# Attention with a gated bilinear branch: masked Q tiles copied out of one SBUF evacuation, and a third quad with four more VectorE tiles

**Chip and metric.** The kernel runs on one core of one Trainium2 chip. The metric is the device time of one execution in microseconds (us), as the median of several executions; a profile of one execution stands beside it. "Span" is the time from the first to the last instruction in a profile; the device time is 1.6 to 1.8 us longer in the profiled runs shown first.

## The reference, cut to what matters

```python
# x: [1, 2048, 512] bf16; 32 heads of 16; F = 1376
g = sigmoid((x * gate_w).sum(-1, keepdims=True))
q, k, v = split(x @ wqkv)                       # per head, Dh = 16
p = softmax(einsum("bhqd,bhkd->bhqk", q, k) * Dh ** -0.5)
a = einsum("bhqk,bhkd->bhqd", p, v) ... @ wo
b = ((x @ w_gate) * (x @ w_up)) @ w_down
return g * a + (1 - g) * b
```

There are 32 heads with 2048 x 2048 scores each. In tiles of 128 keys by 512 queries that makes 2048 tiles whose exponential is wanted. This is most of the work.

## The kernel before

The program is a list scheduler. While it is built, it plays the five engines forward with fixed durations (a "plan") and emits each instruction in the order in which the plan starts it. Each engine's program on the chip is its list in that order, with waits on semaphores in it. So any change of a duration, a buffer or a seed gives a new order of everything.

A "quad" is a group of query block and heads with 64 score tiles (32 quads). ScalarE takes 48 tiles of a quad, as true exps, two or three tiles wide ("pairs" and "triples"). VectorE takes 16: it makes a 16-bit integer approximation straight from PSUM, then VectorE or GpSimd add three constants to it ("shift copies"), and TensorE averages the four versions in the PV product. In the quads of HBQ, VectorE takes 20 and ScalarE 44. The PV product is that of the probabilities with the values. A "bank" is a piece of PSUM that matmuls write, "bank X" the one named psX; an "evacuation" reads a finished result out of it, and this program lets TensorE use it again only after that.

```python
    HBQ = [24, 30]                    # quads in which VectorE takes four more tiles
    NMAIN = 54                        # 128x512 cells for probabilities
...
    # query block: projected into a PSUM bank, evacuated twice, each time times a mask
    for p in range(2):
        ev_q[c, b, p] = add("dve", [last, o_mask] + q_last.get((c - 1, b), []),
            lambda v, p=p: v.tensor_scalar(QM[:, p, b, :], bk.ap, mask[:, p : p + 1], None, ALU.mult),
            0.66, prio=2, cb=lambda k: bk.readers.append(k))
...
    # in gen_step: shift copies of VectorE run when the plan has GpSimd free, and GpSimd waits for them
    if eng in ("dve", "pool") and (best is None or best.prio > CPR):
        if eng == "pool" or lock["pool"] <= t:
            c = try_copy(eng, t)
            if c is not None:
                if eng == "dve":
                    lock["op"] = c
                elif lock["op"] is not None:
                    c.deps.append(lock["op"])
...
    SEED = 3                          # shifts the planned positions of the projections and MLP ("fills")
```

Note what the ordering of shift copies does: GpSimd waits by a semaphore for VectorE's copies (in the profile before 112.4 us in 89 waits, its largest). VectorE does not wait for GpSimd; that side rests on the plan's times alone.

The softmax here doesn't subtract the row's maximum and nothing guards it: scores larger than these inputs give would overflow.

Of the kernel before, what the change touches and what calls it, by code (L numbers as in the profile page):

```python
# [6 lines left out]
BF16 = mybir.dt.bfloat16  # L7
# [189 lines left out]
def _build(nc, A_x, A_wqkv, A_wo, W_gate, W_up, W_down, gate_w, out):  # L197
# [10 lines left out]
    NB = 4  # L208
    FT = (F + 127) // 128
    FW = [min(128, F - 128 * f) for f in range(FT)]  # L210
    NMAIN = 54
    C_V = NMAIN
    C_H = C_V + 4
    C_D = C_H + FT
# [1 line left out]
    NM = NQ * NCH  # L216
    RA = 24
    VW = 18
    HBQ = [24, 30]
    HB = sorted({(m % NQ) // 2 for m in HBQ})  # L220
    XU = {1: 3, 4: 2, 7: 1, 10: 0}
    XI = {1: 0, 4: 1, 7: 2, 10: 3}
# [12 lines left out]
    with ExitStack() as stack:  # L235

        def sb(name, shape, dt):
            return stack.enter_context(nc.sbuf_tensor(name, shape, dt))
# [17 lines left out]
        OX = sb("OX", [128, 2, 512], BF16)  # L256
        hT = sb("hT", [128, FT, 512], BF16)
        usb = sb("usb", [128, 2, 512], BF16)
        ost = sb("ost", [128, 2, D], BF16)
        oraw = sb("oraw", [128, NO, 512], F32)  # L260
        rb = sb("rb", [128, NO, 512], F32)
# [15 lines left out]
        psO = stack.enter_context(nc.psum_tensor("psO", [128, 512], F32))  # L277

        P = _Plan()
        clock = {"pe": 0.9, "act": 0.9, "dve": 0.9, "pool": 0.9, "sp": 0.9}  # L280
        qs = {e: [] for e in clock}

# [28 lines left out]
        def now(eng, deps, fn, occ, **kw):  # L311
            k = _Task(eng, deps, fn, occ, **kw)
            r = ready(k)
            assert r is not None
            return run_task(k, max(clock[eng], r))
# [62 lines left out]
        )  # L378
        m0 = now("dve", [], lambda v: v.memset(mask[:], 0.0), 0.1)
        for j in range(4):  # L380
            m0 = now("dve", [m0], lambda v, j=j: v.memset(mask[32 * j : 32 * j + 16, 0:1], QS), 0.1)
        o_mask = now("dve", [m0], lambda v: v.tensor_scalar(mask[:, 1:2], mask[:, 0:1], -1.0, QS, ALU.mult, ALU.add), 0.1)
        o_one = now("pool", [], lambda g: g.memset(VS[:, :, :, Dh:VW], 1.0), 0.95)
        o_vone = o_one
        o_sel = now("pool", [], lambda g: g.memset(sel[:], 0.0), 0.3)
# [212 lines left out]
        def f_q(c, b, pos):  # L598
            packs = [
                (  # L600
                    lambda bk, kt=kt: col(
                        bk.ap, wq[:, kt, b * 128 : (b + 1) * 128], xT[:, kt, c * 512 : (c + 1) * 512], kt == 0, kt == KD - 1
                    ),
                    PACK,
                    "c",
                )
                for kt in range(KD)
            ]

            def evac(bk, last):  # L610
                bk.need += 2
                for p in range(2):
                    ev_q[c, b, p] = add(
                        "dve",
                        [last, o_mask] + q_last.get((c - 1, b), []),
                        lambda v, p=p: v.tensor_scalar(QM[:, p, b, :], bk.ap, mask[:, p : p + 1], None, ALU.mult),  # L616
                        0.66,
                        prio=2,
                        cb=lambda k: bk.readers.append(k),
                    )  # L620

            def deps():
                if c and not q_done.get((c - 1, b)):
                    return [None]
                return [d_wq[b]] + xdep(c)

            return Fill(f"q{c}{b}", packs, deps, evac, pos)
# [74 lines left out]
        def f_gate(pos):  # L702
            def mk(bk, kt):
                def fn(e, q):
                    return e.matmul(
                        bk.ap[32 * q : 32 * q + 1, :],
                        gw[:, kt : kt + 1],
                        xT[:, kt, q * 512 : (q + 1) * 512],
                        start=(kt == 0),
                        stop=(kt == KD - 1),  # L710
                        tile_position=(0, 32 * q),
                        skip_group_check=True,
                    )

                return pack4(fn)

            packs = [(lambda bk, kt=kt: mk(bk, kt), PACK, "c") for kt in range(KD)]
            grow = ost.rearrange("p a b -> p (a b)").bitcast(F32)

            def evac(bk, last):  # L720
                bk.need += 1
                e0 = None
                e0 = add("dve", [last], lambda v: v.tensor_copy(grow, bk.ap), 0.61, prio=3, cb=lambda k: bk.readers.append(k))
                e1 = add(
                    "sp",
                    [e0],
                    lambda e: e.dma_start(gscr, grow[0:128:32, :]),
                    0.1,
                    lat=3.0,
                    stream="dgl",  # L730
                    dma=True,
                )
                gsrc = bass.AP(gscr.tensor, gscr.offset, [[1, 128], [128, T]])
                e2 = add(
                    "sp",
                    [e1],
                    lambda e: e.dma_start(gex[:, :], gsrc, allow_slow_non_contiguous=True),
                    0.5,
                    lat=9.0,
                    stream="dgl2",  # L740
                    dma=True,
                )
                e3 = add("act", [e2], lambda a: a.activation(gval[:], gex[:], ACT.Exp, scale=-1.0), 0.1, lat=0.33)
                e4 = add("dve", [e3], lambda v: v.tensor_single_scalar(gden[:], gval[:], 1.0, ALU.add), 0.1)
                e5 = add("dve", [e4], lambda v: v.reciprocal(gval[:], gden[:]), 0.1)
                ogate["g"] = add("dve", [e5], lambda v: v.tensor_scalar(omg[:], gval[:], -1.0, 1.0, ALU.mult, ALU.add), 0.1)

            return Fill("gate", packs, lambda: [d_gw] + xt_all + d_x[1:], evac, pos)
# [3 lines left out]
        def f_u(c, f, pos):  # L752
            w = FW[f]
            packs = [
                (
                    lambda bk, kt=kt: col(
                        bk.ap, wu[:, kt, f * 128 : f * 128 + w], xT[:, kt, c * 512 : (c + 1) * 512], kt == 0, kt == KD - 1
                    ),
                    PACK,
                    "c",  # L760
                )
                for kt in range(KD)
            ]
            n = c * FT + f

            def evac(bk, last):
                bk.need += 1
                ocopy[n] = add(
                    "dve",
                    [last, omul.get(n - 2), o_xt[0]],  # L770
                    lambda v: v.tensor_copy(usb[0:w, n % 2, :], bk.ap[0:w, :]),
                    0.6,
                    prio=3,
                    cb=lambda k: bk.readers.append(k),
                )

            def deps():
                if n >= 2 and n - 2 not in omul:
                    return [None]
                return [d_wu] + xdep(c)  # L780

            return Fill(f"u{c}.{f}", packs, deps, evac, pos)

        def f_g(c, f, pos):
# [13 lines left out]
            def evac(bk, last):  # L798
                bk.need += 1
                omul[n] = ev_h[c, f] = add(  # L800
                    "dve",
                    [last, ocopy[n], oend.get((c - 1, 3)), o_xt[0]],
                    lambda v: v.tensor_tensor(hT[0:w, f, :], bk.ap[0:w, :], usb[0:w, n % 2, :], ALU.mult),  # L803
                    0.6,
                    prio=3,
                    cb=lambda k: bk.readers.append(k),
                )

# [12 lines left out]
        def f_d(c, tt, pos):  # L821
# [12 lines left out]
            def evac(bk, last):  # L834
                oend[c, tt] = last
                bk.need += 1
                ev_b[c, tt] = add(
                    "dve",
                    [last, ogate["g"], bfree.get(t - 4) if t < T - 4 else None],
                    lambda v: v.tensor_scalar(b_ap(t), bk.ap, omg[:, t : t + 1], None, ALU.mult),  # L840
                    0.66,
                    prio=3,
                    cb=lambda k: bk.readers.append(k),
                )

# [12 lines left out]
        def combine(t, bank_ap, last, cb=None):  # L858
# [4 lines left out]
                [last, ev_b[c, tt], ogate["g"]] + ([o_out.get(t - 2)] if t < T - 4 else []),  # L863
                lambda v: v.scalar_tensor_tensor(o_dst, bank_ap, gval[:, t : t + 1], b_ap(t), ALU.mult, ALU.add),
                0.66,
                prio=3,
                cb=cb,
            )
            bfree[t] = k
# [196 lines left out]
            return len(pr["p1"]) == len(pr["u"]) and (len(pr["u"]) == 2 or pr.get("last"))  # L1066

        def even(c):
            return len(c) < 3 or all(b - a == c[1] - c[0] for a, b in zip(c, c[1:]))

        def try_copy(eng, t):
            best = None
# [254 lines left out]
        for c in range(NCH - 1):  # L1327
            for b in range(NB):
                fills.append(f_q(c + 1, b, UA0[NQ * c + 2 * b + 2] + 30.0))
        SEED = 3  # L1330
        for i, f in enumerate(fills):
            if f.pos > 0:
                f.pos += ((SEED * 7919 + i * 104729 + SEED * i * 31) % 97) / 97.0 * 6.0 * (SEED > 0)
# [86 lines left out]
        FA1 = 99  # L1420
        LA0 = 0
        LA1 = 1
        XF = -99
        FB = 2
        AOH = 0.057
        M4 = 1
        _build.m4 = 0
# [46 lines left out]
        def pe_step():  # L1474
# [15 lines left out]
            if can and tE <= t:  # L1490
# [24 lines left out]
                        use3 = "d"  # L1515
                if use3 == "d":
                    db.append(s[2])
                if use3 != "f" and bank_free(so[2], t) and lag >= LA1 and not (st["mq"] and so[2] is DB) and st["slot"] == 0:
                    db.append(so[2])
                nmax = 3 if use3 == "a" else 2  # L1520
                djs, dus, dbs = [], [], []
# [67 lines left out]
        def filler(t, can=True):  # L1589
# [22 lines left out]
            if fin and pv is None and st["fill"] is None and wts and fready(wts[0], t):  # L1612
                for bk in tbs:
                    if bank_free(bk, t):
                        start_fill(wts[0], bk, wts)
                        break
            if pv is not None and (nfree < NF or st["fill"] is None or fin):
                do_pv(pv, t)
                return True
            if st["fill"] is not None:  # L1620
# [299 lines left out]
```

## Time and profile before

| | before |
|---|---|
| time, median of 3 | 716.47 us (716.22 to 717.03) |
| profiled execution | 714.12 us, span 712.5 us |
| ScalarE (ACT) busy | 700.3 us, 98% |
| TensorE (PE) busy | 683.8 us, 96% |
| VectorE (DVE) busy | 641.4 us, 90% |
| GpSimd (POOL) busy | 428.4 us, 60% |

The kernel before falls into two groups of times: in 11 executions on one later chip, six lay between 714.1 and 714.9 us and five between 715.6 and 716.0. The profile shows the quicker kind. One thing on record goes with the two groups: in all 31 executions of this kernel in the later rounds, the quicker ones (up to 714.9 us) show a granted TensorE clock of 0.999 or 1.0, the slower ones (715.3 us and more) 0.997 or 0.998. Whether the clock makes the difference was not tested. Some other kernels here show both groups too, so a median can mix them; where it matters, only executions at 0.999 or more are set side by side below.

### The profile page before, as it was taken

How to read it: one execution, taken by the hardware profiler on the slowest of the kernel's cores; microseconds unless marked ns; L12 is line 12 of the kernel's file. 1: busy time of each engine (PE TensorE's matmuls, PEld its weight loads, DVE VectorE, ACT ScalarE, POOL GpSimd, SP SyncE). 2: the span in 40 equal slices, each digit the busy share in tenths (PEclk: the TensorE clock that was granted, in tenths of full speed). 3: DMA queues.
4: the chain of work that ended last, by engine and by line, in shares of the span. 5: the costliest groups of instructions: out<-in, count | busy, mean ns of one | idle time of the engine just before them, and what ended most of it. 6: DMA issues, size and time to landing. Idle time of an engine off the chain costs nothing.

```text
span 712.5 us, 21747 instructions
## 1 busy us (share of the span) xinstructions
PE 683.8 (96%) x9103; PEld 187.7 (26%) x9103; DVE 641.4 (90%) x1215; ACT 700.3 (98%) x689; POOL 428.4 (60%) x467
## 2 busy tenths in 40 slices
PE   8999999999999999999999999999999999999997
PEld 3322333222222222222222222222222222222222
DVE  5999999999998889999988899998889999998897
ACT  7999999999999999999999999999999999999996
POOL 4667676655656665556666565464647656654663
PEclk9999999999999999999999999999999999999999
DMA  6700000100200001000000010000000010000001
GB/s 142 256 7 13 22 18 21 18 17 17 86 21 17 17 8 39 29 17 20 17 3 28 25 40 21 18 6 17 20 18 17 8 37 29 17 19 20 3 21 47
DMA packets 33056, 21.68 MB, mean 30 GB/s; under 512 B 20380, under 2 KB 27964, under 8 KB 32960
## 3 DMA queue, kind: packets, MB, share of 16 engines
q1 hardware_dynamic: 31632, 19.64, 9.4%
q8 instruction: 73, 1.20, 0.7%
q10 hardware_dynamic: 1328, 0.66, 0.4%
q14 instruction: 23, 0.19, 0.1%
HBM read 15.12 MB, written 2.36 MB: 25 GB/s over the span
## 4 chain that ended last, share of the span: by engine, by line
ACT 65%; PE 28%; DVE 4%; issue 2%; POOL 0%; DVEq 0%; ACTq 0%
ACT PT L1656 54%; PE psS L484 10%; PE psO L1190 8%; PE psX L551 8%; ACT wd L1656 4%; ACT wv L1656 4%; ACT hT L1656 2%; DVE PT L1048 1%; PE psS L551 1%; DVE PT L1125 0%; PE psX L640 0%; PE psO L1753 0%; DVE QM L616 0%; PE psX L484 0%; POOL wv L1128 0%
## 5 line engine op out<-in xcount | busy, mean ns | idle before, releaser
L1656 ACT ACTIVATE PT<-psS 128x1024 bf16<-128x1024 f32 (+1 forms) x569 | 617.9, 1386 | 0.2
L1128 POOL TENSOR_SCALAR PT<-PT 128x1024 int16<-128x1024 int16 x214 | 222.2, 1046 | 183.7 <-DVE PT L1125 99.4
L484 PE MATMUL psS<-QM,KE 32*128 32x512 bf16 x1974 | 262.6, 376 | 20.1 <-ACT PT L1656 10.4
L1048 DVE TENSOR_SCALAR PT<-psS 128x512 int16<-128x512 f32 x334 | 226.4, 686 | 29.0 <-PE psS L484 26.6
L1190 PE MATMUL psO<-PT,VS 128*18 128x512 bf16 x1702 | 221.0, 381 | 0.3 <-DVE oraw L1219 0.3
L1190 PE MATMUL psO<-PT,VD 128*18 128x512 bf16 x1168 | 186.7, 381 | 0.6 <-DVE PT L1125 0.6
L990 PEld LDWEIGHTS <-KE 32*128 32x128 bf16 x2048 | 62.3, 91 | 272.5 <-issue 271.1
L1125 DVE TENSOR_SCALAR PT<-PT 128x1024 int16<-128x1024 int16 (+1 forms) x240 | 102.7, 458 | 2.6 <-PE psO L1190 0.8
L1190 PEld LDWEIGHTS psO<-PT,VS 128*18 128x18 bf16 x1702 | 52.0, 88 | 65.6 <-issue 34.7
L551 PE MATMUL psX<-wd,hT 128*32 128x512 bf16 (+1 forms) x704 | 57.2, 385 | 0.0
L1656 ACT ACTIVATE wv<-psS 128x1024 bf16<-128x1024 f32 (+1 forms) x45 | 56.4, 1262 | 0.0
L1128 POOL TENSOR_SCALAR PT<-wv 128x1024 int16<-128x1024 int16 x43 | 44.6, 1046 | 18.2 <-DVE PT L1125 8.9
L1190 PEld LDWEIGHTS psO<-PT,VD 128*18 128x18 bf16 x1168 | 44.3, 88 | 34.6 <-issue 22.1
L551 PE MATMUL psX<-xT,wg 128*32 128x512 bf16 x688 | 52.8, 383 | 0.0
L551 PE MATMUL psX<-xT,wu 128*32 128x512 bf16 x688 | 52.6, 383 | 0.0
L1656 ACT ACTIVATE wd<-psS 128x1024 bf16<-128x1024 f32 (+1 forms) x43 | 50.7, 1275 | 0.0
L1128 POOL TENSOR_SCALAR wv<-PT 128x1024 int16<-128x1024 int16 x36 | 37.7, 1046 | 20.2 <-PE psS L484 6.1
L1048 DVE TENSOR_SCALAR wv<-psS 128x512 int16<-128x512 f32 x68 | 46.0, 686 | 3.3 <-PE psS L484 2.9
L1190 PE MATMUL psO<-wv,VD 128*18 128x512 bf16 x208 | 46.4, 381 | 0.4 <-POOL PT L1128 0.3
L1190 PE MATMUL psO<-wv,VS 128*18 128x512 bf16 x163 | 44.7, 381 | 0.0
L1048 DVE TENSOR_SCALAR PT<-psX 128x512 int16<-128x512 f32 x58 | 39.9, 687 | 5.2 <-PE psS L484 4.8
L803 DVE TENSOR_TENSOR hT<-psX,usb 128x512 bf16<-128x512 f32 (+1 forms) x44 | 30.0, 683 | 6.6 <-PE psX L551 6.3
(128 smaller groups left out, 715.9 us busy)
## 6 DMA issues: line engine op xcount, KB each, us to landing
rb<-rscr SPq DMA_DIRECT2D x31, 256.0 KB
out_dram<-ost SPq DMA_DIRECT2D x12, 128.0 KB, 1.7
wu<-in_B_w_up_dram SPq DMA_DIRECT2D x1, 1376.0 KB, 9.5
wg<-in_B_w_gate_dram SPq DMA_DIRECT2D x1, 1376.0 KB, 12.4
wd<-in_B_w_down_dram SPq DMA_DIRECT2D x1, 1280.0 KB, 6.0
OT<-OX SPq DMA_DIRECT2D x60, 16.0 KB, 1.8
wo<-in_A_wo_dram SPq DMA_DIRECT2D x1, 512.0 KB, 12.9
out_dram<-wk SPq DMA_DIRECT2D x4, 128.0 KB, 1.7
```

The source lines that it names most:

```text
L484: return e.add_instruction(mybir.InstMatmult(name=nc.get_next_instruction_name(), engine=mybir.EngineType.PE, ins=[e.lower_ap(rhs), e.lowe ...
L551: return e.matmul(out_ap[32 * q : 32 * q + w, :], lhs[:, 32 * q : 32 * q + w], rhs, start=s0, stop=s1, tile_position=(0, 32 * q), skip_gro ...
L803: lambda v: v.tensor_tensor(hT[0:w, f, :], bk.ap[0:w, :], usb[0:w, n % 2, :], ALU.mult),
L990: r = e.ldweights(w, tile_position=pos)
L1048: lambda v: v.tensor_scalar(cell_ap(pr["cell"][i : i + 1], mybir.dt.int16), bk.ap, CB, 0.0, ALU.add, ALU.max),
L1125: fn = lambda v: v.tensor_single_scalar(cell_ap(c, I16), cell_ap(src, I16), 32.0 * k, ALU.add)
L1128: fn = lambda g: g.tensor_scalar(cell_ap(c, I16), cell_ap(src, I16), 32.0 * k, 1.0, ALU.add, ALU.mult)
L1190: r = e.matmul(psO[32 * j : 32 * j + VW, :], pv_stationary(m, kt, j, k), cell_ap((cell,)), start=s0, stop=s1, tile_position=(0, 32 * j), s ...
L1656: lambda a: a.activation(cell_ap(c), src, ACT.Exp, scale=LN2 / 128.0),
```

## The change

Its intent: take work from VectorE (one PSUM read per query block in place of two, and short SBUF copies), give the PSUM bank back sooner, and spend the time won on four more tiles in quad 16, which ScalarE then has less.

```diff
-    NMAIN = 54
+    NMAIN = 53
-    HBQ = [24, 30]
+    HBQ = [16, 24, 30]
+        qtmp = sb("qtmp", [128, 512], BF16)
@@ masks are now 1.0 and 0.0, the scale QS is a constant
             def evac(bk, last):
+                if QT and (c or b):
+                    bk.need += 1
+                    e0 = add("dve", [last] + qt_last,
+                        lambda v: v.tensor_single_scalar(qtmp[:], bk.ap, QS, ALU.mult), 0.6, prio=2, ...)
+                    for p in range(2):
+                        ev_q[c, b, p] = add("dve", [e0, o_mask] + q_last.get((c - 1, b), []),
+                            lambda v, p=p: v.tensor_scalar(QM[:, p, b, :], qtmp[:], mask[:, p : p + 1], None, ALU.mult),
+                            0.22, prio=3.2)
+                    return
@@ ... merged shift copies must lie within one buffer; constants LA2, NFD, FP added with the old behaviour
-        SEED = 3
+        SEED = 2
```

qtmp is as large as one of the cells, so there is one cell less. The first of the 16 query blocks is still read twice from PSUM. The new copies are ordinary tasks. They take no part in the ordering of shift copies against GpSimd.

More of the change, by code (lines that the diff above doesn't have):

```diff
@@ L279, in _build @@
         P = _Plan()
+        FP = 3
+        QT = 1
+        qt_last = []
         clock = {"pe": 0.9, "act": 0.9, "dve": 0.9, "pool": 0.9, "sp": 0.9}
@@ L380, in _build @@
         for j in range(4):
-            m0 = now("dve", [m0], lambda v, j=j: v.memset(mask[32 * j : 32 * j + 16, 0:1], QS), 0.1)
-        o_mask = now("dve", [m0], lambda v: v.tensor_scalar(mask[:, 1:2], mask[:, 0:1], -1.0, QS, ALU.mult, ALU.add), 0.1)
+            m0 = now("dve", [m0], lambda v, j=j: v.memset(mask[32 * j : 32 * j + 16, 0:1], 1.0), 0.1)
+        o_mask = now("dve", [m0], lambda v: v.tensor_scalar(mask[:, 1:2], mask[:, 0:1], -1.0, 1.0, ALU.mult, ALU.add), 0.1)
         o_one = now("pool", [], lambda g: g.memset(VS[:, :, :, Dh:VW], 1.0), 0.95)
@@ L610, in evac @@
             def evac(bk, last):
+                if QT and (c or b):
+                    bk.need += 1
+                    e0 = add(
+                        "dve",
+                        [last] + qt_last,
+                        lambda v: v.tensor_single_scalar(qtmp[:], bk.ap, QS, ALU.mult),
+                        0.6,
+                        prio=2,
+                        cb=lambda k: bk.readers.append(k),
+                    )
+                    qt_last.clear()
+                    for p in range(2):
+                        ev_q[c, b, p] = add(
+                            "dve",
+                            [e0, o_mask] + q_last.get((c - 1, b), []),
+                            lambda v, p=p: v.tensor_scalar(QM[:, p, b, :], qtmp[:], mask[:, p : p + 1], None, ALU.mult),
+                            0.22,
+                            prio=3.2,
+                        )
+                        qt_last.append(ev_q[c, b, p])
+                    return
                 bk.need += 2
@@ L615, in evac @@
                         [last, o_mask] + q_last.get((c - 1, b), []),
-                        lambda v, p=p: v.tensor_scalar(QM[:, p, b, :], bk.ap, mask[:, p : p + 1], None, ALU.mult),
+                        lambda v, p=p: v.tensor_scalar(QM[:, p, b, :], bk.ap, mask[:, p : p + 1], QS, ALU.mult, ALU.mult),
                         0.66,
@@ L722, in evac @@
                 e0 = None
-                e0 = add("dve", [last], lambda v: v.tensor_copy(grow, bk.ap), 0.61, prio=3, cb=lambda k: bk.readers.append(k))
+                e0 = add("dve", [last], lambda v: v.tensor_copy(grow, bk.ap), 0.61, prio=FP, cb=lambda k: bk.readers.append(k))
                 e1 = add(
@@ L772, in evac @@
                     0.6,
-                    prio=3,
+                    prio=FP,
                     cb=lambda k: bk.readers.append(k),
@@ L804, in evac @@
                     0.6,
-                    prio=3,
+                    prio=FP,
                     cb=lambda k: bk.readers.append(k),
@@ L841, in evac @@
                     0.66,
-                    prio=3,
+                    prio=FP,
                     cb=lambda k: bk.readers.append(k),
@@ L865, in combine @@
                 0.66,
-                prio=3,
+                prio=FP,
                 cb=cb,
@@ L1068, in even @@
         def even(c):
-            return len(c) < 3 or all(b - a == c[1] - c[0] for a, b in zip(c, c[1:]))
+            g = [sum(x >= lo for lo in (C_V, C_H, C_D)) for x in c]
+            return min(g) == max(g) and c[1] > c[0] and all(b - a == c[1] - c[0] for a, b in zip(c, c[1:]))
         def try_copy(eng, t):
@@ L1422, in _build @@
         LA1 = 1
+        LA2 = 99
         XF = -99
         FB = 2
+        NFD = 18
         AOH = 0.057
@@ L1517, in pe_step @@
                     db.append(s[2])
-                if use3 != "f" and bank_free(so[2], t) and lag >= LA1 and not (st["mq"] and so[2] is DB) and st["slot"] == 0:
+                if use3 != "f" and bank_free(so[2], t) and lag >= (LA1 if st["slot"] == 0 else LA2) and so[2] not in db:
                     db.append(so[2])
@@ L1616, in filler @@
                         break
-            if pv is not None and (nfree < NF or st["fill"] is None or fin):
+            nf = NF if st["fill"] is None or st["fill"].name[0] != "d" else NFD
+            if pv is not None and (nfree < nf or st["fill"] is None or fin):
                 do_pv(pv, t)
```

## The prediction

Passages that told of the hardware what no trace or run of this case shows are cut and marked. "It" in "no case of it to measure" is a VectorE copy held up by a GpSimd instruction, a "collision". In part (a), the 0.133 us for 512 elements are also in the trace of before: the one copy of 2048 elements that ran beside no GpSimd instruction took 0.686 us (at 548.83 us), the median copy of 1024 takes 0.420, and half the difference is 0.133. The second rival is that GpSimd holds up the new copies: of 30, 60% meet a GpSimd instruction and wait half of its 1.046 us; that is the estimate of 9 us. The forecast's sum came to -1.75 - 0.4 + 0.3 = -1.85 us, so 714.6 us. Its last term, +0.3 us for copies held up, was an allowance, not worked out from a trace.

> **What bounds the kernel now.** I read the page first, then ScalarE's instructions grouped by shape, then the order of their starts, and only then the lines that the change touches. The page's first part says that three engines are nearly full, and one is fullest:
>
> ```profile
> PE 683.8 (96%) x9103; PEld 187.7 (26%) x9103; DVE 641.4 (90%) x1215; ACT 700.3 (98%) x689; POOL 428.4 (60%) x467
> ...
> ACT 65%; PE 28%; DVE 4%; issue 2%; POOL 0%; DVEq 0%; ACTq 0%
> ```
>
> ACT is busy 98% of a 712.5 us span and carries 65% of the chain that ended last. PE at 96% is not at a limit by that figure, since ends of matmuls are modelled. The waits settle it: from its first exp to its last, ACT never waits long enough for a wait to be listed; all its listed waits are in the first 8 us or in the tail. Its exps come in two widths, and these are their main groups:
>
> ```profile
> L1656 ACT ACTIVATE PT<-psS 128x1024 bf16<-128x1024 f32 x397 | 420.9, 1259 | 0.2
> L1656 ACT ACTIVATE PT<-psS 128x1536 bf16<-128x1536 f32 x172 | 284.8, 1679 | 0.0
> ```
>
> With the smaller groups (other destination tiles) there are 494 pairs (1024 wide) and 180 triples (1536 wide): 494 x 2 + 180 x 3 = 1528 tiles of 128x512. That is exactly what the program plans for ScalarE: 30 quads of 48 and two of 44. So no tile meant for VectorE was handed back to ScalarE. The durations overlap (420.9 + 284.8 exceeds the busy union of the engine's group, 617.9), so the cost of one exp is the distance between starts. The timeline of ACT gives the ends of the stream:
>
> ```profile
> 8.51 2.85 ACT L1656 ACTIVATE hT<-psS 128x1024 bf16<-128x1024 f32 x3
> ...
> 701.08 1.29 ACT L1656 ACTIVATE wv<-psS 128x1024 bf16<-128x1024 f32 x1
> 702.00 1.71 ACT L1656 ACTIVATE PT<-psS 128x1536 bf16<-128x1536 f32 x1
> 705.40 0.28 ACT L1870 ACTIVATE oraw<-psS 128x128 f32<-128x128 f32 x1 [1.69 <-PE psS L551]
> ```
>
> From 8.51 to 702.00 there are 673 starts. I took the differences of successive starts in the trace and averaged by width: 0.919 us after a pair (median 0.916), 1.338 us after a triple. 494 x 0.919 + 179 x 1.338 = 693.5 us, the whole stretch. The reader should see a stream with no holes: span = 8.5 (head) + 693.5 (exps) + 10.5 (last exp, last PV, output). Only fewer or wider exps, or new holes, can move the time by more than a microsecond.
>
> [...]
>
> [...]
>
> [...] The trace of before has no case of it to measure: the program orders its VectorE and GpSimd shift copies against each other by semaphores, and GpSimd's wait for VectorE's copies is the largest one that it has. The change's new copies do not take part in that ordering.
>
> ```profile
> POOL PT L1128 <- DVE PT L1125: 112.4, 89, 3.5
> ```
>
> **The change, part by part.** (a) Masked Q. Now each of 16 query blocks is evacuated twice from PSUM, each time times a per-partition mask; afterwards 15 blocks are evacuated once with a constant into qtmp, and two SBUF copies apply the mask. The rows that price it:
>
> ```profile
> L616 DVE TENSOR_SCALAR QM<-psX,mask 128x512 bf16<-128x512 f32 x30 | 21.8, 738 | 0.3 <-PE psX L551 0.2
> L616 DVE TENSOR_SCALAR QM<-psS,mask 128x512 bf16<-128x512 f32 x2 | 1.4, 746 | 1.1 <-PE psS L551 1.1
> ...
> L1048 DVE TENSOR_SCALAR PT<-psS 128x512 int16<-128x512 f32 x334 | 226.4, 686 | 29.0 <-PE psS L484 26.6
> L1125 DVE TENSOR_SCALAR PT<-PT 128x1024 int16<-128x1024 int16 x238 | 101.0, 454 | 2.5 <-PE psO L1190 0.8
> ```
>
> Removed: 30 x 0.738 = 22.1 us. Added: 15 x 0.686 (one read of PSUM with constants) = 10.3, and 30 SBUF copies of 512. For these I estimate 0.30 us: the 1024-wide copy less 512 elements[...], 0.454 - 0.133 = 0.32, slightly less because the mean mixes in a few slow ones. 30 x 0.30 = 9.0. VectorE saves 22.1 - 19.3 = 2.8 us. The bank is given back after one read instead of two; in the timeline of VectorE the two reads start 0.65 to 2.5 us apart, so bank X is free some 1.3 us sooner, 15 times. But the profile shows hardly anybody waiting for that: those who waited for L616 are
>
> ```profile
> who waited for it (us, times):
>   PEld psX L705: 0.7, 1
>   PEld psX L551: 0.6, 2
>   PEld psS L640: 0.2, 1
> ```
>
> 1.5 us in all, none of it ACT.
>
> (b) A third quad (number 16) gives four more tiles to VectorE. ScalarE: 1524 tiles. Four tiles less are two pairs, 2 x 0.919 = 1.84 us, or four triples that become pairs, 4 x 0.419 = 1.68 us: 1.75 us off the stream. A check from the two quads that already do this: cutting the stream every 48 (or 44) tiles, quad 24 takes 20.6 us and quad 30 19.7, while their neighbours take 21.4, 21.9, 21.9 and 20.9. Means 20.15 and 21.5: 1.4 us less. VectorE: 4 x 0.686 = 2.7 us of evacuations, and two pairs of tiles need six shift copies; VectorE now makes 426 tile-pair copies of 780 and GpSimd 354, so 3.3 x 0.454 = 1.5 us here and 2.8 us on GpSimd. Sum +4.2 us on VectorE, net of (a) +1.4 us, or 90.2% of the span instead of 90.0%. TensorE: each tile needs four weighted PV products instead of one, 12 more matmuls; at 683.8 us / 9103 = 0.075 us each that is 0.9 us, beside the exps.
>
> (c) The rest. One cell less of 54 in the probability buffer: ACT shows no wait for a cell now, so 0. The seed of the fills' positions shuffles the whole order; it changes how many exps are triples. Three pairs for two triples is 2.757 against 2.676 us, so ten more triples are worth 0.4 us. With bank X free earlier I take ten more: -0.4 us. The stricter test for merged copies touches only four-tile copies, of which there are two now: 0. The two late-stage constants added leave the decisions as they were.
>
> Sum: -1.75 - 0.4 = -2.15 us[...]: 716.5 - 1.9 = 714.6 us.
>
> **The rivals.** First, VectorE's gain is the worth of the change (2.8 us less work should be 2.8 us less time). Against it: ACT does not wait for VectorE anywhere, and VectorE idles 10%. If I am wrong about that, 713 or less.
>
> [...] GpSimd is busy 60% of the time with instructions of 1.046 us; [...] 30 x 0.6 x 0.52 = 9 us on VectorE at worst[...]. It would show as copies of 0.8 to 1.3 us. VectorE's idle 71 us can take it, except where TensorE waits for that very bank and has less than its lead over ACT; if one collision in ten costs ACT 0.2 to 0.5 us, that is under 1 us. If all of it came through, 719 us.
>
> Third, TensorE becomes the bound in the richer quads. The stretches of quads 24 and 30 in the windows view:
>
> ```profile
> 531.90:552.50 20.60, 20.52 (x253) 4.77 (x249) 18.93 (x35) 20.60 (x24) 15.87 (x16) 1.00 0.05 15
> ...
> 661.40:681.10 19.70, 19.64 (x244) 4.59 (x247) 18.29 (x36) 19.70 (x22) 11.77 (x12) 1.00 0.05 16
> ```
>
> The columns are length, then PE, PEld, DVE, ACT and POOL. PE is at 99.6% there, above its 96%, so it has little room; but ACT is full too and the quad is shorter all the same, so PE does not cap it. If quad 16 failed to shorten, 716.5 us: no gain.
>
> **Range and chances.** The sure part is -1.75; the triples may go by +-20, which is +-0.8 us; collisions +0 to +1.5; the executions of before spread by 0.8 us. Together 712.6 to 716.5. A change of 2% is 14 us, eight times the sum, and would need ACT's stream to break up: 0.01 on either side.
>
> **What would show it.** Right: 1524 tiles in ScalarE's exps; distances between starts still 0.919 and 1.338 us; 524 evacuations at line 1048's counterpart; 15 of 0.69 us into qtmp, 30 short copies out of it; head and tail within 0.3 us. The step on copies is wrong if they average well over 0.32 us[...]. The step on composition is wrong if the triples are fewer than 180. The whole is wrong if ACT's starts have holes, that is if the mean distance after a pair rises above 0.925 us, with waits of PE on VectorE ahead of them, or if the tail after the last exp is not 10.5 us.

## The result, and the profile after

The changed kernel took 716.57 us (median of 4, 716.40 to 716.75) against 716.35 us for the kernel before: ratio 1.0007, 95% interval 0.9988 to 1.0027. A ratio here is the mean time of one kernel's runs over that of the other's of the same rounds, so it is not quite the ratio of the medians. Repeated on another chip (r2 below) it was 716.50 against 714.55 us, ratio 1.0019, interval 1.0007 to 1.0031. So the change costs about 0.2% by this ratio, where 0.3% of gain was predicted. All executions of the changed kernel show a clock of 0.999 or more; set against the executions of before on the same chip that do too (714.2 to 714.55 us), it costs 2.0 us, near the 2.1 us between the two spans in the table below. In class it is "same", as forecast with 0.98, but the sign is wrong and the time lies just outside the range.

The page of the changed kernel, busy times and the chain's engines:

```profile
PE 687.3 (96%) x9115; PEld 188.3 (26%) x9115; DVE 648.2 (91%) x1229; ACT 699.9 (98%) x689; POOL 424.7 (59%) x463
...
ACT 48%; PE 37%; DVE 10%; SPq 2%; issue 2%; DMA 0%; POOL 0%; DVEq 0%; POOLq 0%; ACTq 0%
```

ScalarE's part of the chain fell from 65% to 48%, VectorE's rose from 4% to 10%: ScalarE is still the busiest, but other engines now end its waits. The groups by shape of ScalarE's two main forms and of the new VectorE lines (busy us, mean ns, idle before):

```profile
L1685 ACT ACTIVATE PT<-psS 128x1024 bf16<-128x1024 f32 x406 | 424.4, 1234 | 0.6 <-PE psS L488 0.2
L1685 ACT ACTIVATE PT<-psS 128x1536 bf16<-128x1536 f32 x170 | 276.6, 1648 | 0.9 <-PE psS L488 0.8
```

```profile
L630 DVE TENSOR_SCALAR QM<-qtmp,mask 128x512 bf16<-128x512 bf16 x30 | 15.2, 544 | 0.1
L620 DVE TENSOR_SCALAR qtmp<-psX 128x512 bf16<-128x512 f32 x15 | 10.2, 681 | 1.2 <-PE psX L555 1.0
```

For the first time ScalarE waits for scores (L488). The 30 copies out of qtmp average 544 ns, but their median is 346: eight of them took 0.60 to 1.32 us. In the waits view ScalarE has a line that the kernel before does not have, and the timeline shows the end of its stream (the last exp is one tile wide and starts at 704.34):

```profile
ACT PT L1685 <- PE psS L488: 1.0, 3, 0.5
```

```profile
699.44 5.72 ACT L1685 ACTIVATE PT<-psS 128x1536 bf16<-128x1536 f32 x5
707.31 0.28 ACT L1899 ACTIVATE oraw<-psS 128x128 f32<-128x128 f32 x1 [2.15 <-PE psS L555]
```

The listed waits for scores add up to 1.4 us only (0.4 of it on the line of another tile). The distances between starts tell more. I price the stream bare at 0.916 us after a pair (the median of before) and 1.338 us after a triple, and call the rest of the stretch from first to last start the excess. A "hole" is one distance between starts less its bare price.

| us | before | changed (r2) | r5, same order, rows with gaps | r11 |
|---|---|---|---|---|
| first exp starts | 8.51 | 8.60 | 8.60 | 8.88 |
| bare stream | 692.01 | 691.16 | 691.16 | 690.74 |
| excess | 1.48 | 4.59 | 2.80 | 1.74 |
| last start to the end | 10.54 | 10.29 | 10.29 | 11.09 |
| span (sum) | 712.54 | 714.65 | 712.85 | 712.45 |
| pairs, triples, singles | 494, 180, 0 | 496, 177, 1 | 496, 177, 1 | 498, 176, 0 |

The bare stream fell, as intended. The excess rose by 3.1 us and took more than that back. Most of it is a few holes of 0.3 to 0.9 us, at 83.8, 140.4, 185.9, 314.8, 451.5 and 488.6 us in r2 (the late exp's start); the profile first taken has them within 0.1 us of the same places, so they belong to the program and not to chance. Two more of this size, 0.33 us at 21.4 and 0.49 us at 76.4, do not follow a slow copy out of qtmp.

### The profile page after: what moved, and what is told of

It is laid out like the page before. It is cut to its first block, busy times and chain, and to the rows that moved or that the text cites. A ratio compares the mean times of both kernels' runs of the same rounds, so it can differ in the third digit from the quotient of the medians.

```text
span 714.6 us, 21763 instructions
## 1 busy us (share of the span) xinstructions
PE 687.3 (96%) x9115; PEld 188.3 (26%) x9115; DVE 648.2 (91%) x1229; ACT 699.9 (98%) x689; POOL 424.7 (59%) x463
## 4 chain that ended last, share of the span: by engine, by line
ACT 48%; PE 37%; DVE 10%; SPq 2%; issue 2%; DMA 0%; POOL 0%; DVEq 0%; POOLq 0%; ACTq 0%
ACT PT L1685 43%; PE psS L488 12%; PE psO L1216 12%; PE psX L555 9%; ACT wv L1685 4%; DVE PT L1073 2%; SPq L322 2%; DVE PT L1151 2%; ACT wd L1685 1%; DVE wd L1073 1%; PE psX L488 1%; PE psS L555 1%; PE psX L665 1%; DVE QM L630 1%; DVE wd L1151 1%
## 5 line engine op out<-in xcount | busy, mean ns | idle before, releaser
L1154 POOL TENSOR_SCALAR PT<-PT 128x1024 int16<-128x1024 int16 x220 | 228.2, 1047 | 161.7 <-DVE PT L1151 82.7
L488 PE MATMUL psS<-QM,KE 32*128 32x512 bf16 x1968 | 262.8, 376 | 11.2 <-ACT PT L1685 4.0
L1216 PE MATMUL psO<-PT,VS 128*18 128x512 bf16 x1709 | 227.9, 381 | 0.7 <-DVE oraw L1245 0.7
L1216 PE MATMUL psO<-PT,VD 128*18 128x512 bf16 x1231 | 192.3, 381 | 0.6 <-DVE wd L1151 0.6
L1154 POOL TENSOR_SCALAR PT<-wv 128x1024 int16<-128x1024 int16 x57 | 59.1, 1047 | 39.6 <-DVE PT L1151 14.9
L1073 DVE TENSOR_SCALAR wv<-psS 128x512 int16<-128x512 f32 x76 | 51.8, 686 | 6.1 <-PE psS L488 5.6
L1216 PE MATMUL psO<-wv,VS 128*18 128x512 bf16 x182 | 49.9, 381 | 0.1
L1685 ACT ACTIVATE wd<-psS 128x1024 bf16<-128x1024 f32 (+1 forms) x35 | 39.9, 1204 | 0.4 <-PE psS L488 0.4
L1216 PE MATMUL psO<-wv,VD 128*18 128x512 bf16 x167 | 38.2, 381 | 0.0
L1154 POOL TENSOR_SCALAR wv<-PT 128x1024 int16<-128x1024 int16 x24 | 25.1, 1047 | 18.9 <-PE psS L488 4.8
L488 PE MATMUL psX<-QM,KE 32*128 32x512 bf16 x80 | 30.1, 376 | 3.9 <-DVE VS L685 0.9
## 6 DMA issues: line engine op xcount, KB each, us to landing
out_dram<-ost SPq DMA_DIRECT2D x12, 128.0 KB, 1.7
out_dram<-wk SPq DMA_DIRECT2D x4, 128.0 KB, 1.7
```

Source lines behind the costliest of these rows:

```text
L488: return e.add_instruction(mybir.InstMatmult(name=nc.get_next_instruction_name(), engine=mybir.EngineType.PE, ins=[e.lower_ap(rhs), e.lowe ...
L1073: lambda v: v.tensor_scalar(cell_ap(pr["cell"][i : i + 1], mybir.dt.int16), bk.ap, CB, 0.0, ALU.add, ALU.max),
L1154: fn = lambda g: g.tensor_scalar(cell_ap(c, I16), cell_ap(src, I16), 32.0 * k, 1.0, ALU.add, ALU.mult)
L1216: r = e.matmul(psO[32 * j : 32 * j + VW, :], pv_stationary(m, kt, j, k), cell_ap((cell,)), start=s0, stop=s1, tile_position=(0, 32 * j), s ...
L1685: lambda a: a.activation(cell_ap(c), src, ACT.Exp, scale=LN2 / 128.0),
```

## The experiments

Theory: a copy out of qtmp that meets a GpSimd instruction is blocked until that instruction ends (eight copies of 0.60 to 1.32 us where the median is 0.346), and what VectorE does next comes too late for TensorE and so for ScalarE. In the expectations the name of this theory and the reason given for it are cut, since no trace shows that reason; after such a mark stands what the theory led to. Rivals: the new order of work makes the holes by itself; the third quad overloads VectorE or TensorE; the kernel before is an order that came out luckily well.

**r2, the changed kernel again, on the chip of r1, r3 and r4.**

> The changed kernel once more on this chip, as the base for the three others. Expected 716.6 within 0.5 us, the same holes in ScalarE's stream at the same places (81.8, 138.6, 184.2, 312.8, 449.3, 486.6 us) [...].

Measured: 716.50 us (before 714.55 us), the same holes at the same places, so not from chance (the expectation names the start of the exp before each hole), the same slow copies. This is the base for what follows. The tile view of qtmp gives the spread of the copies (duration in ns as least/median/most):

```profile
L630 DVE TENSOR_SCALAR QM<-qtmp,mask x30: 339/346/1315, 37.9 to 570.8; 128x512 bf16<-128x512 bf16 x30
```

Set against GpSimd's instructions one by one, the trace of r2 is sharper still. In ten of the 30 copies a GpSimd instruction was running when the copy began: these took 0.525 to 1.315 us, and every one ended 0.146 to 0.152 us after that instruction. In the other 20 none was running: these took 0.339 to 0.350 us.

The hole before 314.8 us can be followed through four engines in the timeline (start, length, instruction; in brackets the idle time before it and what ended that):

```profile
311.79 1.04 POOL L1154 TENSOR_SCALAR wv<-wv 128x1024 int16<-128x1024 int16 x1 [0.57 <-DVE wv L1073]
...
311.55 1.43 DVE L630 TENSOR_SCALAR QM<-qtmp,mask 128x512 bf16<-128x512 bf16 x2
312.90 0.67 DVE L1073 TENSOR_SCALAR PT<-psX 128x512 int16<-128x512 f32 x1
...
313.63 0.83 PE L555 MATMUL psX<-xT,wg 128*32 128x512 bf16 x12 [0.53 <-DVE PT L1073]
...
314.82 1.45 ACT L1685 ACTIVATE PT<-psS 128x1536 bf16<-128x1536 f32 x1 [0.30 <-PE psS L488]
```

GpSimd starts at 311.79, just before the second copy (311.81). The first copy has taken 0.34 us, the second takes 1.17 and ends 0.15 us after GpSimd's instruction. The evacuation of bank X behind it starts at 312.90, TensorE waits 0.53 us for that bank before the MLP matmuls, the next scores stand behind those in TensorE's order, and ScalarE's exp starts 0.66 us late. The other five holes have the same chain: in each, the evacuation of bank X stands close behind the slow copy, and TensorE waits for it (0.70 us at 82.78, 0.45 at 139.22, 0.37 at 184.47, 0.74 at 450.31, 0.49 at 487.37).

**r1, the copies in another layout, first attempt (failed as an experiment).**

> The changed kernel with every engine's instructions in the same order; only the 30 masked copies differ: 514 columns, the output written as 257 rows of 2[...] (result stays right). [...] the copies that took 1.12 to 1.32 us (9 of 30 were over 0.5 us, mean 0.544) fall to one value, about 0.45 to 0.5 us, none over 0.6; the holes in ScalarE's stream 0.3 to 0.9 us wide that follow the blocked copies (6 of them, 3.4 us in all) vanish, and the time falls by 2 to 3.5 us against the changed kernel, to about 713.5. Rival (the new order of the work, or the third quad, makes the holes): the copies may change, the holes stay within 0.1 us each, time within 0.7 us of the changed kernel's 716.6.

The layout was to keep the copies from being blocked; why it should was not shown. The trace has one run of 514 on both sides of the copy: the rows touched and had been merged. So the form of the copies was not changed, they still took up to 1.45 us, and the holes stayed. Time 716.96 us, ratio 1.0028 (1.0016 to 1.0041). It tells only that the holes come back with the order.

**r5, the copies in rows with gaps between them.**

The edit, cut to what matters:

```diff
-        qtmp = sb("qtmp", [128, 512], BF16)
+        qtmp = sb("qtmp", [128, 65, 9], BF16)       # 65 rows of 8, one element between
-        QM = sb("QM", [128, 2, NB, 512], BF16)
+        QM = sb("QM", [128, 2, NB, 520], BF16)      # 8 columns of padding, not used
-   v.tensor_scalar(QM[:, p, b, :], qtmp[:], mask...)
+   v.tensor_scalar(QM[:, p, b, :], qtmp[:, :, 0:8], mask...)
```

> The first attempt at this failed: its output rows touched, were merged into one run, and the copies kept their form (its trace has one run of 514 on both sides, and the same 1.1 us copies). Now qtmp is laid out as 65 rows of 8 with a gap between rows, and the copy writes one run of 520[...]. Order of all engines as in the changed kernel, result right. [...] all 30 copies within 0.1 us of each other, about 0.45 us (none over 0.6), holes after 81, 138, 184, 312, 449 and 486 us gone (each under 0.1), stream of exps 2.5 to 3.5 us shorter than the changed kernel's 694.4 us, time 713 to 714. Rival (order of the work): the copies even out but the holes stay, time 716 to 717.

The instruction lists of all engines are the changed kernel's, but for one memset of 9 columns at the start. (The stream of the changed kernel is 695.8 us from first to last start, not 694.4 as the expectation has it.) The tile view of qtmp:

```profile
L630 DVE TENSOR_SCALAR QM<-qtmp,mask x30: 500/506/517, 37.8 to 569.1; 128x520 bf16<-128x520 bf16 x30
```

All 30 copies take one time. Each undisturbed copy is 0.16 us slower than before (506 against 346 ns), and none is blocked, though GpSimd was running when 12 of them began. The expectation's 0.45 us had no measurement behind it, and why this layout escapes the blocking is not shown. The time is 715.14 us against 714.58 for the kernel before, ratio 1.0009 (0.9996 to 1.0021), where r2 had 1.0019. These two intervals overlap; the executions at a clock of 0.999 or more do not: 714.65 to 715.14 us here, 716.30 to 716.69 in r2 (another chip, with the same time for the kernel before). The same place as above, in its timeline:

```profile
310.97 0.93 DVE L630 TENSOR_SCALAR QM<-qtmp,mask 128x520 bf16<-128x520 bf16 x2
311.82 0.68 DVE L1073 TENSOR_SCALAR PT<-psX 128x512 int16<-128x512 f32 x1
...
312.55 0.83 PE L555 MATMUL psX<-xT,wg 128*32 128x512 bf16 x12
```

TensorE no longer waits there. The six named holes shrank from 3.41 us in all (0.52, 0.47, 0.33, 0.66, 0.87, 0.56) to 0.02, 0.26, under 0, 0.16, 0.16 and 0.07, by 2.7 us in all. The excess fell by 1.79 us, less than the 2.5 to 3.5 that I had expected of the stream, since small holes opened elsewhere (nineteen above 0.1 us against seventeen; new ones of 0.12 to 0.20 us at 119.1, 264.2, 348.2 and 571.2). That the slower copies opened them is likely and not shown. And 0.24 us of the fall lies at 21.4 us, before the first copy out of qtmp: that is chance. The time missed the expected 713 to 714. The sign and the theory held, the expected size was too large.

**r6, GpSimd gives way.** After planning, eight GpSimd instructions that had overlapped slow copies get one more dependency, on the second masked copy of that block; the order on each engine stays.

```diff
+        for k, i in {59: 3, 79: 5, 134: 9, 157: 11, 229: 17, 312: 23, 332: 25, 350: 27}.items():
+            pool_ops[k].deps.append(masked_copies[i])
```

> The changed kernel with every engine's order kept; eight GpSimd instructions that in the changed kernel's trace overlapped a slow masked copy now wait for the second masked copy of that block. So GpSimd gives way, not VectorE. [...] masked copies all about 0.34 us (perhaps one or two still blocked at a new place), six large holes gone, GpSimd a little later, time 713 to 714.5. Rival (VectorE is not what makes the holes, or GpSimd's lateness costs the same): time 716 to 717.

```profile
L630 DVE TENSOR_SCALAR QM<-qtmp,mask x30: 334/344/353, 38.0 to 569.8; 128x512 bf16<-128x512 bf16 x30
...
  POOL PT L1154: 4.2, 2
```

```profile
449.25 0.39 PE L1216 MATMUL psO<-PT,VS 128*18 128x512 bf16 x2 [0.64 <-POOL PT L1154]
```

No copy is blocked now (at most 353 ns). GpSimd waits 8.2 us for them (4.2, 2.1, 1.1 and 0.8 by tile). Time 715.61 us, ratio 1.0011 (0.9997 to 1.0024), worse than the 713 to 714.5 expected. The excess is 3.57 us: five of the six named holes are gone. One is left at 0.66 us (450.7), with another cause: TensorE now waits 0.64 us for the delayed GpSimd copy, the second line above. A new pair of 0.71 and 0.28 us stands at 68.6 to 69.8 us, just after GpSimd had been made to wait, beside two shift copies of 1.05 and 1.25 us. So the lateness can be moved to GpSimd, but there it is not free.

**r3 and r4, new orders with the seed of the changed kernel.** In r3 the builder itself orders the copies against GpSimd:

```diff
+                if k.lk and lock["pool"] > t:
+                    continue
...
+            if best.lk:
+                lock["op"] = best
+                lock["dve"] = clock["dve"]
```

> The changed kernel, but its builder lets the masked copies run only when GpSimd is planned to be free and makes GpSimd's next work wait for them, as it already does for the shift copies. The whole order changes. [...] copies at 0.34 us with at most two or three over 0.6; few holes over 0.3 us; 713 to 715 us. Rival: holes as many as in the changed kernel, 716 to 717.5.

Measured: 720.50 us, ratio 1.0078 (1.0064 to 1.0092). Two copies were over 0.6 us (0.75 at most), as the theory said, but the excess was 6.07 us, one hole alone 1.99 at 698.9 us, and the stretch from last start to end 12.72. In r4 QT is 0: third quad, but both masked reads from PSUM.

> The changed kernel with both masked reads again from PSUM (third quad, seed and buffer count stay as changed). The whole order changes. [...] no holes from copies, but VectorE has 3 us more work: 714 to 716. If instead the third quad overloads VectorE or TensorE, 717 or more, with holes in the quads 16, 24 and 30.

Measured: 722.91 us, ratio 1.0109 (1.0096 to 1.0122). The excess was only 2.59 us; the loss is in the stretch from last start to end, 17.45 us, with 40 PV matmuls started after the last exp had ended (3 in the kernel before). Both times lie 5 us or more above what the theory expected; r4's is in the range of its rival, but without the rival's holes in the three quads. The reason could be read before the next runs: the builder's plan itself, printed when the kernel is built, ended 5.9 us later for r3 and 8.8 us later for r4 than for the changed kernel. Both had been planned with a seed chosen for another program. So neither tells the theories apart, and a comparison of orders needs a seed chosen for each.

**r7 and r8, the same two with seeds chosen by plan** (15 of 24 tried, and 3; r8 and r10 also keep the 53 cells of the changed kernel).

> The version whose builder orders the masked copies against GpSimd (720.5 us before), with the seed of the fills' positions that its own plan likes best of 24 (its plan ends 4.7 us earlier than with seed 2, and 0.5 us earlier than the plan of the kernel before). If the seed decides as much as the change, it gains 4 to 5 us on r3 and lands at 715 to 716.5; if it lands under 714 it beats both kernels.

> The third quad alone, masked reads from PSUM as in the kernel before, with seed 3 (the seed of the kernel before; its plan ends 6.5 us earlier than with seed 2, 0.6 us later than the plan of the kernel before). If r4 was slow only through its seed: 715 to 717, tail near 9 us in place of 17.3. If the third quad itself overloads VectorE: still over 719.

Both 716.30 us: ratio 1.0022 (1.0010 to 1.0035) and 1.0023 (1.0010 to 1.0035). The seed was worth 4.2 and 6.6 us. r7 had one slow copy (0.99 us), an excess of 3.01 us and 11.89 us after the last start: an order with one blocked copy can have as much excess, so the collisions are one cause of holes and not the only one. r8, the third quad without qtmp, had an excess of 2.05 us, so the third quad does not break up the stream; but the stretch after the last start was 12.93 us against 10.54, with 24 PV matmuls after the last exp. The third quad alone gained nothing in this order. That the work which qtmp would have saved on VectorE comes back at the end is a reading, not tested.

**r9, the kernel before with another seed.**

> The kernel before with nothing changed but the seed of the fills' positions (8 in place of 3; its plan ends 0.3 us earlier than the plan of the kernel before). If the kernel before is an order that happened to come out well on the chip, this one, equally good on paper, is 1 to 2.5 us slower: 715.5 to 717, with more than 1.5 us of excess in ScalarE's stream or a longer tail. If orders of equal plan are equal on the chip: 714 to 715.

Measured: 714.86 us against 714.87, ratio 0.9998 (0.9985 to 1.0011); excess 1.64 us. So the kernel before need not be a lucky order: the one other order tried, with a plan as good, is as good on the chip.

**r10, qtmp without the third quad** (the other half of the change, best seed of 100 by plan).

```diff
-    HBQ = [16, 24, 30]
+    HBQ = [24, 30]
-        SEED = 2
+        SEED = 70
```

> The copies out of qtmp without the third quad: two quads with four more VectorE tiles, 1528 tiles on ScalarE, the best seed of 100 by plan (0.6 us before the plan of the kernel before). [...] again some 6 to 10 of 30 copies blocked to 1.1 us, 2 to 3 us of holes: 716 to 718. If the third quad is what costs, and not the copies: 713.5 to 715.

```profile
L630 DVE TENSOR_SCALAR QM<-qtmp,mask x30: 333/349/1316, 38.4 to 568.9; 128x512 bf16<-128x512 bf16 x30
```

Measured: 720.31 us, ratio 1.0072 (1.0059 to 1.0085), beyond the expected 716 to 718. Ten copies were over 0.6 us, eight of them over 1.1. The excess was 6.03 us, and the stretch after the last start 10.50, as in the kernel before. In the first half of the run the holes stand at the places of the changed kernel (84.2, 140.9, 186.3, 315.3 us); the three blocks with copies over 1.1 us in the second half are each followed by holes: 0.85, 0.39 and 0.46, and 1.25 us. So the holes come with the copies, without the third quad; r8 had the third quad and not the copies, and not these holes.

**r11 and r12, the copies laid out as in r5 (rows with gaps), planned at 0.37 us each, two seeds.**

> The changed kernel [...] planned at 0.37 us each as they were measured, best seed of 100 by its plan (0.3 us later than the changed kernel's plan). Copies all near 0.5 us; stream 691 to 692.5 us without the copies' holes; 713 to 715. Under 714 it beats both kernels.

> As r11 with the second best seed (its plan ends 0.2 us later). 713 to 715.5; the difference from r11 shows how far two orders of nearly equal plan differ on the chip.

```profile
L630 DVE TENSOR_SCALAR QM<-qtmp,mask x30: 422/508/517, 38.1 to 571.0; 128x520 bf16<-128x520 bf16 x30
```

714.22 us (ratio 0.9995, 0.9983 to 1.0008) and 714.60 us (0.9994, 0.9981 to 1.0007) against 714.87. The excess is 1.74 and 1.40 us. These are the full change without the collisions (the plan's 0.37 us is a price for the order; the trace has 0.508). Both beat the changed kernel by their ratios to the kernel before (1.0019), though from other rounds; neither is told apart from the kernel before. The best version here is a draw. Their excess is near that of the kernel before (1.48), so what r5 keeps above that belongs to the order of the changed kernel and not to the change as such.

The builder's plan (no measurement, but its printed end) makes a last check, since its fixed durations have no blocked copies in them. The measured span exceeds the plan's end by 3.1 us (before), 3.9 (r9), 4.4 (r11), 4.7 (r12), 4.6 (r8), 4.4 (r4) and 4.7 (r3, two slow copies), 5.2 (r5, whose plan is the changed kernel's), 5.6 (r7, one slow copy), 6.0 (r6, GpSimd made to wait), 7.0 (changed, eight slow copies) and 8.7 (r10, ten). r1, with eight slow copies, is 7.9 behind. The three with eight or ten slow copies fall furthest behind the plan; among the rest, with none to two, the order is not that of their number.

## Why the prediction was wrong

**What bounds the kernel** was read rightly: ScalarE's stream sets the time, VectorE's own sum does not. r5 shows it sharply: the median copy got slower by 0.16 us, and the stream of exps shorter by 1.8 us.

**Part (a), the saving on VectorE**, failed in one term, the price of the copies. The 15 evacuations took 0.681 us as priced (0.686). The undisturbed copies took 0.346 us where I had estimated 0.30. The trace of before could have led there: I priced them from shift copies, which add a constant, but these multiply by a mask read per partition, and from PSUM that costs 0.738 against 0.681 us. The median shift copy (0.420), less the 0.133 for 512 elements (half its distance from the 0.686 of the copy of 2048) and plus this 0.057, is 0.344, an estimate from these rows; no run measured the price of the mask out of SBUF. But the mean was 0.544: blocked copies cost 30 x (0.544 - 0.346) = 5.9 us, and VectorE's busy time rose from 641.4 to 648.2 us, where I had +1.4 us. The bank given back sooner was worth nothing that can be seen: the listed waits of TensorE's matmuls for bank X went from 0.9 us in the kernel before to 7.6 in r2, 5.8 in r5 and 1.9 in r11.

**Part (b), four tiles**: 1524 tiles in ScalarE's exps, 12 more matmuls on TensorE (9115), as stated. Quad 16 took 20.09 us in r2 against 21.32 before, cut at whole exps as in the prediction; with the exps that straddle a cut shared out it is 20.10 against 21.78, and quads 24 and 30 of before take 20.1 each, so the prediction's check of 1.4 us a quad was low. It did shorten, and the third rival (TensorE as the bound) falls. Of the 1.75 us, 0.85 came in the stream and 0.25 after its last start: the last exp has one tile in place of three, so two of the four tiles were saved at the very end, where the rest of the PV product (12 matmuls after the last exp, against 3) fills the time.

**Part (c), the composition**: I took ten more triples, -0.4 us. There were three fewer. The sum of (b) and (c) was to be -2.15 and is -1.10 (692.01 to 691.16, and 10.54 to 10.29). This is the smaller of the two errors.

**The second rival was right and mis-sized.** The 9 us "at worst" on VectorE were 5.9, and ten copies collided where the estimate has 30 x 0.6 = 18. The step that failed is the next: that one collision in ten costs ScalarE 0.2 to 0.5 us, +0.3 us in the sum. Not one in ten but seven of the ten blocked copies (two of them in one block) had a hole of 0.33 to 0.87 us behind them, six holes and 3.41 us in all. With the same order and no collisions 1.79 us of the excess of 3.11 us over before is gone; that is shown. The other 1.3 us stays in r5 and is not there in r11 and r12, so it goes with the order of work; what in the order makes it was not tried. It stands mostly between 76 and 145 us, where TensorE still waits for bank X (0.74 us at 84.9, 0.55 at 108.3, 0.57 at 128.0). One hole there (0.38 us at 76.2) follows a shift copy of 1.19 us at 72.69 that overlapped a GpSimd instruction. That other shift copies do the same is argued, not shown.

Behind it lies a sentence that was wrong: that the trace of before has no case of a collision to measure. It had 39, of 422 shift copies 1024 wide: over 0.55 us where the median is 0.42, each with a GpSimd instruction running when it began, 13.7 us of blocking in all. All 39 ended 0.278 to 0.283 us after that instruction, as regular as the copies out of qtmp. One of them, in the timeline of the kernel before:

```profile
116.28 1.45 DVE L1125 TENSOR_SCALAR wd<-PT 128x1024 int16<-128x1024 int16 x2
...
115.85 1.27 POOL L1251 TENSOR_TENSOR OX<-oraw,rb 128x512 bf16<-128x512 f32 x1
```

The first of the two copies took 1.117 us and ended 0.28 us after GpSimd's instruction. I had seen that the mean of 454 ns "mixes in a few slow ones" and had not asked what they were. Asked, the trace would have given the share of copies that are held up (9% with the one-sided ordering) and the length of a block. It would also have shown that such blocks do not always hurt: 13.7 us of blocking went with an excess of only 1.48 us. The masked copies are worse placed: in all six holes they stand ahead of the evacuation that frees the bank TensorE needs next.

The sign that the prediction named for holes would have missed them: the mean distance after a pair is 0.9165 us in r2, under its 0.925. Nearly all of the excess stands after triples, whose mean distance rose from 1.338 to 1.363 us.

**The base.** I added a difference worked out on a profile of 714.12 us to a median of 716.47 us, which by its size looks like the slower group (these three executions have no clock on record). A range wider by a microsecond would have held the time, and the sign would still have been wrong: 1.9 us of gain were predicted, and at a like clock the change cost 2.0 us.

## What to carry to other kernels

Here a SBUF to SBUF copy of 512 elements took 0.34 to 0.35 us alone and 0.525 to 1.315 us when a GpSimd instruction was running as it began (r2). Before adding one, look at the spread of the copies that are already there, not at their mean, and ask what stands behind it in the queue. And where a program's order is planned, a new operation must enter every rule the plan has for its kind (here the ordering against GpSimd), and two variants can be compared only after each has had its own search for an order.
